# The first MoE's inner blocks 4 to 11 by pairs, four of them through seven half-depth products

## The chip, the cores and the metric

One core of a Trainium2 chip runs the whole program. The time is device microseconds (us) of one execution, and of several executions the median. TensorE (PE) does the matmuls, VectorE (DVE), ScalarE (ACT) and GpSimd (POOL) the rest, and SyncE (SP) starts the transfers.

## The reference

Attention over 2 batches of 8 heads of 768 positions (each position sees the first four and a window of 128) gives x, 1536 tokens by 512. Two feed-forward layers follow, whose weights are float64:

```python
def _moe_ref(x, w_gate, w_val, w_out) -> np.ndarray:
    g = x @ w_gate
    silu = g * (1.0 / (1.0 + np.exp(-g)))
    val = x @ w_val
    return (silu * val @ w_out).astype(np.float32)
...
def _moe2_ref(x, w_in, w_out, alpha) -> np.ndarray:
    h = x @ w_in
    g = np.maximum(h, 0.0) + alpha * np.minimum(h, 0.0)
    return (g @ w_out).astype(np.float32)
```

The inner size is 1536 in the first layer (12 inner blocks of 128) and 2048 in the second (16 inner blocks).

## The kernel before

**Arithmetic.** A product of full precision is made of three matmuls in a shorter format: high by high, high by low, low by high. So each operand is held as a high and a low tile. A product of 512 channels with one inner block for 512 tokens (`proj`) is 12 matmuls of 128x128 by 128x512; one of half the channels (`Duo.product`) is 6.

**Weights.** `Stream` turns float64 weights into high and low tiles, item by item (an item is 128x512 weights). SP loads raw words into one of RB = 3 buffers. `start` takes the upper words' magnitude on ACT (Abs, L548), `bits` puts the float32 together with three DVE operations (L584, L587, L590), ACT rounds it to the high tile wh (L593), and `low` subtracts for the low tile wl (L599), on POOL where `idle_pool` is set and on DVE elsewhere. Each item moves one step at each `tick`, and a tick follows each `yield` of a unit. An item's tiles lie in one of WB = 12 slots, with WX = 7 more while the third token block of chunk 0 and chunk 1 run. Items of kind 2 and 3 are sums of the two items ahead of them: four POOL operations on 128x256 halves (L566 to L569), wh by ACT (L572), wl by POOL.

**First layer.** `Moe1.unit(c, b)` does chunk c of four inner blocks for token block b of three (512 tokens each): for two blocks at a time the gate products with Silu on ACT, then the value products, each multiplied with its gate on DVE (`hid`, L718) and split into `hh` (ACT, L679) and `hl` (DVE, L680); then four output products of 12 matmuls, `po`, added to the running sum by DVE (L742; in chunk 0 copied by ACT). Units (0, 0) and (0, 1) run beside attention, whose DVE order is fixed by the code (`tc.manual_schedule`).

**Second layer.** `Duo` takes its inner blocks by pairs. After a plain first pair, the products with token blocks 0 and 1 follow a scheme of 2x2 blocks (halves of the channels, two inner blocks or two token blocks) with seven products in place of eight: it needs sums of weights (kinds 2 and 3) and sums of the tokens' values t1 to t4 (`Duo.sums`, DVE on 128x1024, L827). ACT copies some products out of PSUM (`keep`, L850), and DVE adds them to others (L855). Token block 2 is done plainly. Then 12 output products of 6 matmuls follow (`pf`, L947 to L949, added by DVE at L954).

**Order.** A scheduler sets each engine's order from the order of the code and estimated times; each engine then runs its list in order, held up only by what an instruction needs. PSUM has eight banks of 128x512.

Of the kernel before, what the change touches and what calls it, by code (L numbers as in the profile page):

```python
# [35 lines left out]
WB = 12  # L36
WX = 7
RB = 3
VB = 6
LAG = 2  # L40
ORDER = ((0, 3), (1, 2), (4, 5))
# [18 lines left out]
def setup(nc, tc, ctx, g):  # L60
    const = ctx.enter_context(tc.tile_pool(name="const", bufs=1))
    g.const = const
    g.ident = const.tile([P, P], F32, name="ident")
    for nm in ("alpha", "sig", "sal", "sdn"):
        setattr(g, nm, const.tile([P, NF2], F32, name=nm))
    g.mask_a = const.tile([P, KW], F32, name="mask_a")
    g.mask_b = const.tile([P, KW], F32, name="mask_b")
    g.mask_0 = const.tile([P, P], F32, name="mask_0")
    g.mask_1 = const.tile([P, 2 * P], F32, name="mask_1")
    g.above = const.tile([P, P], I32, name="above")  # L70
    g.zero = const.tile([P, T], mybir.dt.bfloat16, name="zero")
# [397 lines left out]
def weight_pools(nc, tc, ctx, g, sfx):  # L469
# [31 lines left out]
class Stream:  # L501
# [49 lines left out]
    def bits(self):  # L551
# [9 lines left out]
        if kind > 1:  # L561
# [10 lines left out]
            nc.scalar.activation(wh, m, AF.Copy)  # L572
# [5 lines left out]
        if slot is None or g.exact:  # L578
            nc.vector.tensor_scalar(out=m, in0=m, scalar1=WMAX, scalar2=-WMAX, op0=ALU.min, op1=ALU.max)
            w2 = g.w2_p.tile([P, KD * P], F32, tag="w2", name="w_2")  # L580
            sign, wi = mi, w2.bitcast(I32)
# [49 lines left out]
def moe1_seq(wg, wv, wo):  # L631
    seq = []
    for c in range(NF1 // CHUNK):
# [17 lines left out]
def duo_seq(wi, wo):  # L651

    seq = []
    for f in range(0, NF2, DUO):
        fs = range(f, f + DUO)
        seq += [(0, wi, x, DOWN, 3 * NF1 + x) for x in fs]
        seq += [(2, None, 0, None, None), (3, None, 0, None, None)] if f else []
# [153 lines left out]
class Duo:  # L811
# [3 lines left out]
    def __init__(self, nc, g, st, base, ys, out, halves):  # L815
        self.nc, self.g, self.st, self.base, self.ys, self.out, self.halves = nc, g, st, base, ys, out, halves
        self.accs = {}

    def sums(self, a0, a1):

        nc, g = self.nc, self.g
        a, b, c, d = a0[:, 0:2], a0[:, 2:4], a1[:, 0:2], a1[:, 2:4]
        t1, t2, t4 = ([half(g.x_p2, n + z) for z in "hl"] for n in ("t1", "t2", "t4"))
        self.ts = ts = [t1, t2, [y[0] for y in self.ys[1]], t4]

        def sub(out, x, y):
            return lambda: nc.vector.tensor_tensor(out=out, in0=x, in1=y, op=ALU.subtract)  # L827

        def split(x, t):
            return lambda: split_hidden(nc, x, *t)  # L830

        self.last = split(c, ts[2])
        return [sub(a, c, a), sub(c, d, c), split(a, ts[0]), sub(d, d, a), split(d, ts[1]), sub(b, b, d), split(b, ts[3])]
# [14 lines left out]
    def keep(self, ps, tag):  # L848
        t = self.g.u_p.tile([P, T], F32, tag=tag, name=tag)
        self.nc.scalar.activation(t, ps, AF.Copy)  # L850
        return t

    def add(self, ps, u):
        t = self.g.t_p.tile([P, T], F32, tag="hid", name="sum")
        self.nc.vector.tensor_tensor(out=t, in0=ps, in1=u, op=ALU.add)  # L855
        return t

    def bend(self, src, f, pair, inplace=False):
        nc, g = self.nc, self.g
        if inplace:  # L860
            hid = src
            nc.vector.scalar_tensor_tensor(
                out=hid, in0=src, scalar=g.alpha[:, f:f + 1], in1=src, op0=ALU.mult, op1=ALU.max
            )
        else:
            neg = g.t_p.tile([P, T], F32, tag="sg", name="neg")
            nc.scalar.activation(neg, src, AF.Copy, scale=g.alpha[:, f:f + 1])
            hid = g.t_p.tile([P, T], F32, tag="hid", name="hid2")
            nc.vector.tensor_tensor(out=hid, in0=src, in1=neg, op=ALU.max)
        split_hidden(nc, hid, *(t[:, f % 2] for t in pair))  # L870

    def plain(self):

        st, w, hids = self.st, self.base, {}
        for b, pool in ((0, None), (1, self.g.h_p2), (2, None)):
            hids[b] = hidden_pair(self.g, pool)
            for r in range(DUO):
                ph = self.new("ph")
                proj(self.nc, ph, st.get(w + r), *self.ys[b])
                self.bend(ph, r, hids[b])  # L880
                yield
            if b == 1:
                self.last()
        st.done(DUO)
        for b in range(3):
            for _ in self.outputs(0, b, w + DUO, *hids[b]):
                yield
        st.done(DUO)

    def unit(self, c):  # L890
        nc, g, st = self.nc, self.g, self.st
        if c == 0:
            yield from self.plain()
            return
        w = self.base + 2 * DUO + (c - 1) * 3 * DUO
        f = c * DUO
        (y0h, y0l), (y1h, y1l), y2 = self.ys
        b11, b21, b22 = (y0h[0], y0l[0]), (y0h[1], y0l[1]), (y1h[1], y1l[1])
        t1, t2, t3, t4 = self.ts
        hids = {0: hidden_pair(g)}  # L900
        pa, pb, pc = self.new("pa"), self.new("pb"), self.new("pc")
        self.product(pa, w, 0, b11, True)
        p1 = self.keep(pa, "p1")
        yield
        self.product(pc, w, 1, b21, True)
        self.bend(self.add(pc, p1), f, hids[0], True)
        yield
        self.product(pb, w + 2, 0, t1, True)
        yield
        self.product(pa, w + 2, 1, t2, False)  # L910
        u2 = self.keep(pa, "u2")
        yield
        hids[2] = hidden_pair(g)
        hids[1] = hidden_pair(g, g.h_p2)
        for r in range(DUO):
            ph = self.new("ph")
            proj(nc, ph, st.get(w + r), *y2)
            self.bend(ph, f + r, hids[2])
            yield
            if r == 0:  # L920
                self.product(pa, w + 3, 0, t3, False)
                u3 = self.keep(pa, "u3")
                self.bend(self.add(pb, u3), f + 1, hids[1], True)
                yield
        self.product(pa, w + 1, 1, t4, False)
        self.bend(pa, f + 1, hids[0])
        yield
        self.product(pb, w + 3, 1, b22, False)
        self.bend(self.add(pb, u2), f, hids[1], True)
# [243 lines left out]
```

## Time and profile before

| | |
|---|---|
| median of 3 runs | 670.21 us (668.44 to 671.4) |
| profiled execution, its own time | 670.04 us |
| its span in the trace | 668.0 us |
| what lies around the span | 2.04 us |
| PE busy | 648.6 us, 3056 matmuls |
| DVE / ACT / POOL busy | 430.7 / 306.6 / 158.6 us |
| mean granted clock of TensorE | 0.983 of full speed |

The span runs from the first to the last recorded instruction of the core; own time is that of the same execution measured outside. The busy time of an engine is the sum of its instructions; it says which engine is nearly full, and the waits and the chain that ended last say whether it also sets the time.

### The profile page before, as it was taken

Reading aid. Unit: us, or ns where it says so; the run is one execution under the profiler, and the core shown is the slowest. Engines: PE = TensorE matmul, PEld = TensorE weight load, DVE = VectorE, ACT = ScalarE, POOL = GpSimd, SP = SyncE. Lnnn points to the kernel's source line nnn. Section 1 sums busy time; section 2 is a strip of 40 time slices with the busy share of each in tenths; the row PEclk is TensorE's granted clock in tenths of the full one; section 3 lists DMA queues with packets and bytes.
Section 4 is the critical chain, followed back from the end, with each engine's and each line's share of the span. In section 5 each row is a group of like instructions: output and inputs, shape, how many; then the busy total and the mean of one; then the engine's idle time right before and its main releaser. Section 6 shows DMA issues by size and latency. Waiting matters only on the chain.

```text
span 668.0 us, 8689 instructions
## 1 busy us (share of the span) xinstructions
PE 648.6 (97%) x3056; PEld 511.6 (77%) x3056; DVE 430.7 (64%) x915; ACT 306.6 (46%) x714; POOL 158.6 (24%) x203
## 2 busy tenths in 40 slices
PE   8879899999999999999999999999999999999996
PEld 4547566767788888888888888888888888888884
DVE  6897967355189852227432699938686969684654
ACT  4768755666366622024222356655344353533040
POOL 3547644334100000000000004614334251420000
PEclk8879899999999999999999999999999999999999
DMA  8754444100045620001300023222121303100005
GB/s 288 221 171 149 154 136 149 32 13 1 1 135 181 187 97 0 1 1 40 118 0 1 0 94 99 82 66 72 64 65 62 95 31 95 32 1 1 0 1 193
DMA packets 37203, 52.29 MB, mean 78 GB/s; under 512 B 4384, under 2 KB 28960, under 8 KB 37152
## 3 DMA queue, kind: packets, MB, share of 16 engines
q1 hardware_dynamic: 34944, 51.65, 24.2%
q8 instruction: 26, 0.43, 0.3%
q10 hardware_dynamic: 2208, 0.01, 0.2%
q14 instruction: 25, 0.20, 0.1%
HBM read 48.51 MB, written 3.15 MB: 77 GB/s over the span
## 4 chain that ended last, share of the span: by engine, by line
PE 88%; DVE 5%; ACT 3%; issue 1%; DMA 1%; POOL 1%; ACTq 0%; POOLq 0%
PE pf L947 7%; PE pf L948 7%; PE pf L949 7%; PE pa L841 6%; PE po L735 5%; PE pg L666 5%; PE po L736 5%; PE po L737 5%; PE pv L666 5%; PE pg L667 5%; PE pg L668 5%; PE pv L668 5%; PE pv L667 5%; PE pb L841 3%; PE ph L667 3%; PE ph L666 3%
## 5 line engine op out<-in xcount | busy, mean ns | idle before, releaser
L599 POOL TENSOR_TENSOR wl<-w_m,wh 128x512 fp32r<-128x512 f32 x44 | 57.9, 1322 | 99.1 <-ACT wh L593 87.1
L593 ACT ACTIVATE wh<-w_m 128x512 fp32r<-128x512 f32 x68 | 42.6, 629 | 76.9 <-PE pf L949 45.4
L947 PE MATMUL pf<-wh,hh 128*128 128x512 f32 x192 | 74.7, 389 | 0.0
L948 PE MATMUL pf<-wl,hh 128*128 128x512 f32 x192 | 74.7, 389 | 0.0
L679 ACT ACTIVATE hh<-hid 128x512 fp32r<-128x512 f32 x63 | 39.9, 633 | 66.7 <-DVE hid L718 51.7
L566 POOL TENSOR_TENSOR w_raw<-w_m 128x256 f32<-128x256 f32 x7 | 5.9, 840 | 253.0 <-DVE w_m L590 226.9
L949 PE MATMUL pf<-wh,hl 128*128 128x512 f32 x192 | 62.0, 389 | 0.0
L954 DVE TENSOR_TENSOR acc<-pf,acc 128x512 f32<-128x512 f32 x84 | 54.4, 681 | 11.4 <-PE pf L949 10.7
L718 DVE TENSOR_TENSOR hid<-pv,sg 128x512 f32<-128x512 f32 x36 | 24.7, 687 | 56.6 <-PE pv L668 56.5
L680 DVE TENSOR_TENSOR hl<-hid,hh 128x512 fp32r<-128x512 f32 x63 | 47.4, 754 | 20.7 <-ACT hh L679 20.3
L666 PE MATMUL pg<-xh,wh 128*128 128x512 f32 x144 | 57.5, 400 | 0.0
L666 PE MATMUL pv<-xh,wh 128*128 128x512 f32 x144 | 56.9, 395 | 0.0
L548 ACT ACTIVATE w_m<-w_raw 128x512 f32<-128x512 f32 x68 | 45.8, 674 | 24.0 <-DVE wl L599 9.6
L667 PE MATMUL pg<-xl,wh 128*128 128x512 f32 x144 | 56.7, 393 | 0.0
L668 PE MATMUL pg<-xh,wl 128*128 128x512 f32 x144 | 56.6, 393 | 0.0
L735 PE MATMUL po<-hh,wh 128*128 128x512 f32 x144 | 56.4, 395 | 0.0
L668 PE MATMUL pv<-xh,wl 128*128 128x512 f32 x144 | 56.1, 390 | 0.0
L667 PE MATMUL pv<-xl,wh 128*128 128x512 f32 x144 | 56.1, 389 | 0.0
L736 PE MATMUL po<-hh,wl 128*128 128x512 f32 x144 | 56.0, 390 | 0.0
L737 PE MATMUL po<-hl,wh 128*128 128x512 f32 x144 | 53.3, 390 | 0.0
L587 DVE SCALAR_TENSOR_TENSOR w_m<-w_raw,w_m 128x512 int32<-128x512 int32 x68 | 50.0, 736 | 1.1
L590 DVE SCALAR_TENSOR_TENSOR w_m<-w_raw,w_m 128x512 uint32<-128x512 uint32 x68 | 49.0, 723 | 0.6
(161 smaller groups left out, 1400.6 us busy)
## 6 DMA issues: line engine op xcount, KB each, us to landing
w_raw<-in_moe_w_out SPq DMA_DIRECT2D x28, 512.0 KB, 3.4
w_raw<-in_moe_w_in SPq DMA_DIRECT2D x16, 512.0 KB, 3.8
w_raw<-in_moe_w_gate SPq DMA_DIRECT2D x12, 512.0 KB, 4.4
w_raw<-in_moe_w_val SPq DMA_DIRECT2D x12, 512.0 KB, 4.4
th<-in_qk SPq DMA_DIRECT2D x16, 336.0 KB, 3.3
vr<-in_v SPq DMA_DIRECT2D x16, 192.0 KB, 2.6
out<-acc SPq DMA_DIRECT2D x12, 256.0 KB, 2.5
th<-in_qk SPq DMA_DIRECT2D x8, 256.0 KB, 5.1
```

Of the source, the lines that this page charges most:

```text
L599: eng.tensor_tensor(out=wl, in0=m, in1=wh, op=ALU.subtract)
L666: nc.tensor.matmul(ps, wh[:, c], chan(xh, kk), start=(kk == 0), stop=False)
L667: nc.tensor.matmul(ps, wh[:, c], chan(xl, kk), start=False, stop=False)
L668: nc.tensor.matmul(ps, wl[:, c], chan(xh, kk), start=False, stop=(kk == KD - 1))
L735: nc.tensor.matmul(ps, wh[:, mc], hh, start=(x == 0), stop=False)
L736: nc.tensor.matmul(ps, wl[:, mc], hh, start=False, stop=False)
L737: nc.tensor.matmul(ps, wh[:, mc], hl, start=False, stop=(x == CHUNK - 1))
L841: self.nc.tensor.matmul(ps, a[:, c], m[:, k], start=(start and k == 0 and y == 0), stop=(k == 1 and y == 2), skip_group_check=True)
L947: nc.tensor.matmul(ps, hh[:, x, ts], wh, start=(x == 0), stop=False)
L948: nc.tensor.matmul(ps, hh[:, x, ts], wl, start=False, stop=False)
L949: nc.tensor.matmul(ps, hl[:, x, ts], wh, start=False, stop=(x == DUO - 1))
L954: nc.vector.tensor_tensor(out=av, in0=ps, in1=av, op=ALU.add)
```

## The change

Chunk 0 of the first layer (blocks 0 to 3) stays. Blocks 4 to 11 are done by pairs (`Duo1`): 4, 5 and 10, 11 plainly, 6, 7 and 8, 9 with the seven products, once for the gates and once for the values (`Chain`, which the second layer now uses too, in the order ORDER7). This needs x's sums t1 to t4 once (`Duo1.sums`, taken up one by one at the yields of the third token block of chunk 0), and two items more (kinds 2 and 3) ahead of each of the four chains. The outputs are added up by pairs, so each of the 12 sums of a token block takes its additions pair by pair. The high tiles of the weights' sums come from POOL instead of ACT, in both layers, and `idle_pool` stays set, so the low tiles of the first layer's later items come from POOL too. Slots are 10, with 2 more for chunk 0's items and 2 more from the last pair on. `g.soon()` gives a higher priority in the scheduler to what follows a product: the copies and additions of the chains, Silu, multiply, split, and the additions of the outputs. Masks and scratch tiles of attention move to pools that close with it. The diff, cut to its core (the second layer's class is the same as before but for `Chain` and `g.soon()`):

```diff
+ORDER7 = (1, 2, 5, 6, 8, 7, 9, 4, 3)
-WB = 12
-WX = 7
+WB = 10
 RB = 3
+WA = 2
...
-            nc.scalar.activation(wh, m, AF.Copy)
+            nc.gpsimd.tensor_copy(wh, m)
             self.halves = (i, m, wh, wl)
...
+SUMS = [(2, None, 0, None, None), (3, None, 0, None, None)]
+def duo1_seq(wg, wv, wo):
+    seq = []
+    for f in range(CHUNK, NF1, DUO):
+        fs = range(f, f + DUO)
+        more = SUMS if CHUNK < f < NF1 - DUO else []
+        seq += [(0, wg, x, DOWN, x) for x in fs] + more
+        seq += [(0, wv, x, DOWN, NF1 + x) for x in fs] + more
+        seq += [(1, wo, x, DOWN, 2 * NF1 + x) for x in fs]
+    return seq
...
+        with self.g.soon():
+            self.nc.scalar.activation(t, ps, AF.Copy)
...
+class Chain:
+    def __init__(self, duo, w, ops, more, room, sink):
+        self.duo, self.w, self.ops, self.more, self.room, self.sink = duo, w, ops, more, room, sink
+    def plus(self, ps, u, b, r):
+        t = self.room(b, r)
+        with self.duo.g.soon():
+            self.duo.nc.vector.tensor_tensor(out=t, in0=ps, in1=u, op=ALU.add)
+        self.sink(b, r, t, True)
+    def step(self, x):
+        d, w = self.duo, self.w
+        b11, b21, b22, t1, t2, t3, t4 = self.ops
+        if x == 1:
+            self.a = d.new("pa")
+            d.product(self.a, w, 0, b11, True)
+            self.p1 = d.keep(self.a, "u1")
+        elif x == 2:
+            ps = d.new("pc")
+            d.product(ps, w, 1, b21, True)
+            self.plus(ps, self.p1, 0, 0)
+        elif x == 6:
+            d.product(self.a, w + 2, 1, t2, False)
+            self.u2 = d.keep(self.a, "u2")
+        elif x == 5:
+            self.b = d.new("pb")
+            d.product(self.b, w + 2, 0, t1, True)
+        elif x == 7:
+            d.product(self.a, w + 3, 0, t3, False)
+            self.plus(self.b, d.keep(self.a, "u1"), 1, 1)
+        elif x == 4:
+            d.product(self.a, w + 1, 1, t4, False)
+            self.sink(0, 1, self.a, False)
+        elif x == 3:
+            d.product(self.b, w + 3, 1, b22, False)
+            self.plus(self.b, self.u2, 1, 0)
+        else:
+            ps = d.new("ph")
+            proj(d.nc, ps, d.st.get(w + x - 8), *self.more)
+            self.sink(2, x - 8, ps, False)
...
+    def sums(self):
         nc, g = self.nc, self.g
+        (x0h, x0l), (x1h, x1l), _ = self.xs
+        a, c, d = ((x[0], y[0]) for x, y in ((x0h, x0l), (x1h, x1l), (x1h[1:], x1l[1:])))
+        b = x0h[1], x0l[1]
+        t1, t2, t4 = ([half(g.x_p2, n + z) for z in "hl"] for n in ("t1", "t2", "t4"))
+        self.ops = [a, b, d, t1, t2, None, t4]
+        u, v = (g.h_p2.tile([P, 2, T], F32, tag=z, name="tsum") for z in ("hh", "hl"))
+        return [
+            self.sub(u, c[0], a[0]), self.add(u, u, c[1]), self.sub(u, u, a[1]),
+            self.sub(v, d[0], u), self.split(u, t1), self.add(v, v, d[1]),
+            self.sub(u, b[0], v), self.split(v, t2), self.add(u, u, b[1]),
+            self.sub(v, d[0], c[0]), self.split(u, t4), self.add(v, v, d[1]), self.sub(v, v, c[1]), lambda: self.third(v),
+        ]
+    def third(self, v):
+        self.ops[5] = [half(self.g.x_p3, "t3" + z) for z in "hl"]
+        split_hidden(self.nc, v, *self.ops[5])
...
+        def gate(b, r, src, own):
+            t = src if own else room_g(b, r)
+            with g.soon():
+                nc.scalar.activation(t, src, AF.Silu)
+            gates[b, r] = t
+        def room_v(b, r):
+            return g.t_p.tile([P, T], F32, tag="hid", name="hid")
+        def value(b, r, src, own):
+            hid = src if own else room_v(b, r)
+            with g.soon():
+                nc.vector.tensor_tensor(out=hid, in0=src, in1=gates[b, r], op=ALU.mult)
+                split_hidden(nc, hid, *(t[:, r] for t in pairs[b]))
...
+        last = (NF1 - CHUNK) // DUO - 1
+        w = self.base + (3 * DUO + (c - 1) * 5 * DUO if c else 0)
+        if c in (0, last):
+            yield from self.plain(w, c == last)
+            return
+        pairs = self.pairs()
+        room_g, gate, room_v, value = self.sinks(pairs)
+        for i, room, sink in ((0, room_g, gate), (2 * DUO, room_v, value)):
+            chain = self.chain(w + i, self.ops, self.xs[2], room, sink)
+            yield from chain.steps(ORDER7)
+            chain.done()
+        for b in (2, 0, 1):
+            for m in range(KD):
+                self.output(b, m, w + 4 * DUO, *pairs[b])
+                yield
+        self.st.done(DUO)
+    def output(self, b, m, w, hh, hl, y=None):
+        nc, st = self.nc, self.st
+        mc = slice(m * P, (m + 1) * P)
+        ps = self.new("po")
+        for x in range(DUO):
+            wh, wl = st.get(w + x)
+            nc.tensor.matmul(ps, wh[:, mc], hh[:, x], start=(x == 0), stop=False)
+            nc.tensor.matmul(ps, wl[:, mc], hh[:, x], start=False, stop=False)
+            nc.tensor.matmul(ps, wh[:, mc], hl[:, x], start=False, stop=(x == DUO - 1))
+        av = self.accs[b][0][:, m]
+        with self.g.soon():
+            nc.vector.tensor_tensor(out=av, in0=ps, in1=av, op=ALU.add)
+            if y:
+                split_hidden(nc, av, *(chan(t, m) for t in y))
...
+    seq = moe1_seq(w_gate, w_val, w_out, 1) + duo1_seq(w_gate, w_val, w_out)
+    base = len(seq)
+    add_pool(nc, tc, early, g.w_ps, "w_pa", WA, "right")
...
+    for nm, bufs in (("x_p2", 6), ("u_p", 1), ("h_p2", 1), ("t_p2", 4)):
+        setattr(g, nm, ctx.enter_context(tc.tile_pool(name=nm, bufs=bufs)))
+    st.idle_pool = True
...
+    later.extend(d1.sums())
+    run([m1.unit(0, 2)])
+    assert g.w_ps.pop()[1] == WA
+    early.close()
+    last = (NF1 - CHUNK) // DUO - 1
     with ExitStack() as inner:
-        add_pool(nc, tc, inner, g.w_ps, "w_p2", WX)
-        run([m1.unit(0, 2)] + [m1.unit(1, b) for b in range(NPASS)])
-        assert g.w_ps.pop()[1] == WX
-    for nm, bufs in (("x_p2", 6), ("u_p", 1), ("h_p2", 1)):
-        setattr(g, nm, ctx.enter_context(tc.tile_pool(name=nm, bufs=bufs)))
-    run([m1.unit(2, b) for b in range(NPASS)])
-    st.idle_pool = True
-    run([m2.unit(c) for c in range(NF2 // DUO)])
-    assert asked
+        g.x_p3 = inner.enter_context(tc.tile_pool(name="x_p3", bufs=2, side="right"))
+        run([d1.unit(c) for c in range(last)])
+        assert not later
+    add_pool(nc, tc, ctx, g.w_ps, "w_p3", WA, "right")
+    st.own = range(base - 3 * DUO, len(st.seq))
+    run([d1.unit(last)] + [d2.unit(c, ys) for c in range(NF2 // DUO)])
...
+        g.soon = lambda: tc.high_priority(offset=SOON)
```

DVE at the end of attention and the start of unit (0, 2): `xl` is the low part of attention's last values, `tsum` the sums of x, `t1l` and `t2l` their low parts, `w_m` and `wl` the weights. Before:

```order
L1019 TENSOR_TENSOR xl<-xp,xh 128x256 x3
L599 TENSOR_TENSOR wl<-w_m,wh 128x512 x2
L584 TENSOR_SCALAR w_m<-w_m 128x512
L587 SCALAR_TENSOR_TENSOR w_m<-w_raw,w_m 128x512
L584 TENSOR_SCALAR w_m<-w_m 128x512
L590 SCALAR_TENSOR_TENSOR w_m<-w_raw,w_m 128x512
L587 SCALAR_TENSOR_TENSOR w_m<-w_raw,w_m 128x512
L590 SCALAR_TENSOR_TENSOR w_m<-w_raw,w_m 128x512
L599 TENSOR_TENSOR wl<-w_m,wh 128x512 x2
L584 TENSOR_SCALAR w_m<-w_m 128x512
L718 TENSOR_TENSOR hid<-pv,sg 128x512
```

With the change (line numbers there are of the changed kernel):

```order
L1182 TENSOR_TENSOR xl<-xp,xh 128x256 x2
L833 TENSOR_TENSOR tsum<-xh 128x1024
L1182 TENSOR_TENSOR xl<-xp,xh 128x256
L836 TENSOR_TENSOR tsum<-tsum,xl 128x1024
L833 TENSOR_TENSOR tsum<-tsum,xl 128x1024
L833 TENSOR_TENSOR tsum<-xh,tsum 128x1024
L693 TENSOR_TENSOR t1l<-tsum,t1h 128x1024
L836 TENSOR_TENSOR tsum<-tsum,xl 128x1024
L833 TENSOR_TENSOR tsum<-xh,tsum 128x1024
L731 TENSOR_TENSOR hid<-pv,sg 128x512
L836 TENSOR_TENSOR tsum<-tsum,xl 128x1024
L693 TENSOR_TENSOR t2l<-tsum,t2h 128x1024
```

In this place the weights' bit operations and low tiles gave way to the sums of x; the bit operations stand behind them, and the low tiles have left DVE's list.

POOL behind its last work for attention (the rows `pt<-pt`). Before, it had nothing until the second layer's first sums of weights:

```order
L295 AFFINE_SELECT pt<-pt 128x2x128 x2
L566 TENSOR_TENSOR w_raw<-w_m 128x256
L567 TENSOR_TENSOR w_raw<-w_raw,w_m 128x256
L568 TENSOR_TENSOR w_m<-w_m 128x256
L569 TENSOR_TENSOR w_m<-w_m,w_raw 128x256
L599 TENSOR_TENSOR wl<-w_m,wh 128x512 x3
```

With the change:

```order
L296 AFFINE_SELECT pt<-pt 128x2x128 x2
L599 TENSOR_TENSOR wl<-w_m,wh 128x512 x7
L567 TENSOR_TENSOR w_raw<-w_m 128x256
L599 TENSOR_TENSOR wl<-w_m,wh 128x512
L568 TENSOR_TENSOR w_raw<-w_raw,w_m 128x256
L569 TENSOR_TENSOR w_m<-w_m 128x256
L570 TENSOR_TENSOR w_m<-w_m,w_raw 128x256
L573 CAST wh<-w_raw 128x512
L573 CAST wh<-w_m 128x512
```

Low tiles and four groups of sums of the first layer now stand ahead of the second layer's.

ACT from the copies of unit (0, 2)'s outputs (`acc`) on: Abs of an item writes `w_m,wsum`, `sg` is Silu, `hh` the high part of the product of gate and value. Before:

```order
L740 ACTIVATE acc_2255<-po 128x512
L548 ACTIVATE w_m,wsum<-w_raw 128x512
L593 ACTIVATE wh<-w_m 128x512
L710 ACTIVATE sg<-pg 128x512
L548 ACTIVATE w_m,wsum<-w_raw 128x512
L593 ACTIVATE wh<-w_m 128x512
L710 ACTIVATE sg<-pg 128x512
L548 ACTIVATE w_m,wsum<-w_raw 128x512
L593 ACTIVATE wh<-w_m 128x512
L679 ACTIVATE hh<-hid 128x512
```

With the change:

```order
L753 ACTIVATE acc_2227<-po 128x512 x3
L593 ACTIVATE wh<-w_m 128x512 x2
L957 ACTIVATE sg<-ph 128x512 x2
L549 ACTIVATE w_m,wsum<-w_raw 128x512
L692 ACTIVATE hh<-hid 128x512 x2
L549 ACTIVATE w_m,wsum<-w_raw 128x512
L957 ACTIVATE sg<-ph 128x512 x2
L692 ACTIVATE hh<-hid 128x512 x2
```

Between two Abs there now stand the high parts and Silus of a pair, and one Abs still stands ahead of each of the first high parts.

## Rows read from the trace of the kernel before

**Rows 1.** The page's first part: span, and each engine's busy time, share, instructions.

```profile
span 668.0 us, 8689 instructions
...
PE 648.6 (97%) x3056; PEld 511.6 (77%) x3056; DVE 430.7 (64%) x915; ACT 306.6 (46%) x714; POOL 158.6 (24%) x203
```

**Rows 2.** All waits of PE between 100 and 700 us (total, times, longest).

```profile
PE ps_s L224 <- ACT pr L234: 0.8, 1, 0.8
PE xp L320 <- POOL pt L295: 0.4, 1, 0.4
```

**Rows 3.** Busy time by stage (PE, PEld, DVE, ACT, POOL; then clock, DMA, GB/s).

```profile
0.00:182.00 182.00, 169.01 (x941) 114.98 (x942) 114.81 (x414) 113.72 (x352) 82.76 (x137) 0.94 0.38 121
182.00:215.00 33.00, 33.00 (x148) 27.28 (x147) 29.58 (x53) 22.20 (x47) 0.00 (x0) 1.00 0.46 146
215.00:345.00 130.00, 130.00 (x575) 107.67 (x574) 63.21 (x104) 38.02 (x73) 0.00 (x0) 1.00 0.19 61
345.00:400.00 55.00, 55.00 (x245) 45.53 (x244) 32.10 (x48) 21.07 (x37) 0.05 (x1) 1.00 0.08 24
400.00:661.00 261.00, 261.00 (x1154) 216.02 (x1153) 190.30 (x299) 111.58 (x207) 75.77 (x66) 1.00 0.19 60
```

**Rows 4.** The chain that ended last, 600 us on (start, length, instruction).

```profile
630.31 1.36 PE pa L841 x6
...
661.62 0.69 DVE acc L954
```

**Rows 5.** Groups of instructions by line (busy, mean ns, idle before and releaser).

```profile
L599 POOL TENSOR_TENSOR wl<-w_m,wh 128x512 fp32r<-128x512 f32 x44 | 57.9, 1322 | 99.1 <-ACT wh L593 87.1 <-PE pf L949 11.4
...
L599 DVE TENSOR_TENSOR wl<-w_m,wh 128x512 fp32r<-128x512 f32 x31 | 21.0, 685 | 2.1 <-ACT wh L593 1.9
L742 DVE TENSOR_TENSOR acc<-po,acc 128x512 f32<-128x512 f32 x24 | 15.8, 686 | 24.1 <-PE po L737 23.8
L295 POOL TENSOR_SCALAR_AFFINE_SELECT pt<-pt 128x256 f32<-128x256 f32 x32 | 13.7, 450 | 0.3
...
L855 DVE TENSOR_TENSOR sum<-pb,u 128x512 f32<-128x512 f32 x14 | 9.6, 686 | 6.7 <-ACT u L850 6.7
...
L850 ACT ACTIVATE u<-pa 128x512 f32<-128x512 f32 x14 | 8.3, 593 | 9.2 <-PE pa L841 9.2
L568 POOL TENSOR_TENSOR w_m<-w_m 128x256 f32<-128x256 f32 x7 | 8.1, 1154 | 0.2
...
L567 POOL TENSOR_TENSOR w_raw<-w_raw,w_m 128x256 f32<-128x256 f32 x7 | 6.6, 938 | 0.1
L566 POOL TENSOR_TENSOR w_raw<-w_m 128x256 f32<-128x256 f32 x7 | 5.9, 840 | 253.0 <-DVE w_m L590 226.9 <-PE pa L841 26.1
L569 POOL TENSOR_TENSOR w_m<-w_m,w_raw 128x256 f32<-128x256 f32 x7 | 5.7, 808 | 0.0
...
L827 DVE TENSOR_TENSOR acc<-acc,acc 128x1024 f32<-128x1024 f32 x3 | 3.7, 1218 | 0.0
```

**Rows 6.** DVE's groups between 182 and 215 us, the columns as in 5.

```profile
L587 DVE SCALAR_TENSOR_TENSOR w_m<-w_raw,w_m 128x512 int32<-128x512 int32 x11 | 7.6, 689 | 0.2
L590 DVE SCALAR_TENSOR_TENSOR w_m<-w_raw,w_m 128x512 uint32<-128x512 uint32 x10 | 6.8, 684 | 0.0
L584 DVE TENSOR_SCALAR w_m<-w_m 128x512 int32<-128x512 int32 x11 | 4.7, 424 | 1.9 <-ACT w_m L548 1.9
```

**Rows 7.** Timeline around 428 us (start, length, instruction, idle before and releaser).

```profile
425.74 0.67 ACT L548 ACTIVATE w_m<-w_raw 128x512 f32<-128x512 f32 x1 [2.17 <-POOL w_m L568]
...
427.62 1.82 POOL L599 TENSOR_TENSOR wl<-w_raw,wh 128x512 fp32r<-128x512 f32 x1 [1.21 <-PE pf L949]
...
428.20 1.79 DVE L590 SCALAR_TENSOR_TENSOR w_m<-w_raw,w_m 128x512 uint32<-128x512 uint32 x1
```

**Rows 8.** Timeline around 454 us, the columns as in 7.

```profile
452.99 0.63 ACT L679 ACTIVATE hh<-hid 128x512 fp32r<-128x512 f32 x1 [0.76 <-DVE hid L869]
...
454.58 0.39 PE L947 MATMUL pf<-wh,hh 128*128 128x512 f32 x1
```

More of the change, by code (lines that the diff above doesn't have):

```diff
@@ L579, in bits @@
             nc.vector.tensor_scalar(out=m, in0=m, scalar1=WMAX, scalar2=-WMAX, op0=ALU.min, op1=ALU.max)
[L580 to L581 removed]
+            sign, wi = mi, hi
         else:
@@ L628, in done, with moe1_seq @@
             self.n_done += 1
-def moe1_seq(wg, wv, wo):
+def moe1_seq(wg, wv, wo, chunks=NF1 // CHUNK):
     seq = []
-    for c in range(NF1 // CHUNK):
+    for c in range(chunks):
         fs = range(c * CHUNK, (c + 1) * CHUNK)
@@ L811, with __init__, sub, add @@
 class Duo:
[L815 to L833, printed above, removed]
+    def __init__(self, nc, g, st):
+        self.nc, self.g, self.st = nc, g, st
+    def sub(self, out, x, y):
+        return lambda: self.nc.vector.tensor_tensor(out=out, in0=x, in1=y, op=ALU.subtract)
+    def add(self, out, x, y):
+        return lambda: self.nc.vector.tensor_tensor(out=out, in0=x, in1=y, op=ALU.add)
+    def split(self, x, t):
+        return lambda: split_hidden(self.nc, x, *t)
     def product(self, ps, w, r, x, start):
@@ L849, in keep @@
         t = self.g.u_p.tile([P, T], F32, tag=tag, name=tag)
-        self.nc.scalar.activation(t, ps, AF.Copy)
-        return t
[L853 to L858, printed above, removed]
-        nc, g = self.nc, self.g
[L860 to L864, printed above, removed]
-        else:
[L866 to L929, printed above, removed]
-        st.done(2 * DUO)
-        yield
-        for b in (2, 0, 1):
-            for _ in self.outputs(c, b, w + 2 * DUO, *hids[b]):
-                yield
@@ new lines, in keep, with chain, pairs, steps @@
+        with self.g.soon():
+            self.nc.scalar.activation(t, ps, AF.Copy)
+        return t
+    def chain(self, w, ops, more, room, sink):
+        return Chain(self, w, ops, more, room, sink)
+    def pairs(self):
+        g = self.g
+        return {b: hidden_pair(g, pool) for b, pool in ((0, g.h_p), (2, g.h_p), (1, g.h_p2))}
+class Chain:
[36 more added lines that the diff above has]
+            self.sink(2, x - 8, ps, False)
+    def steps(self, order):
+        for x in order:
+            self.step(x)
+            yield
+    def done(self):
+        self.duo.st.done(2 * DUO)
```

139 lines of the change are left out of this document (115 added, 24 removed).

## The prediction, made before the changed kernel ran

> **What bounds the kernel now.** The page's first part comes first: PE is busy for 648.6 of 668.0 us, DVE for 430.7 [rows 1]. A share alone does not say that an engine sets the end, so the waits of PE are next: between 100 and 700 us there are two, 1.2 us in all, both on work of attention [rows 2]. The table by stage says the same from the other side: from 182 to 661 us PE's busy time equals the length of each stretch, at a granted clock of 1.00 in each (2.4 GHz), while DVE has spare time in all of them: 3.4 us of 33 just behind attention, 67 of 130 later, 71 of 261 in the second layer [rows 3]. The chain that ended last runs from 600 us to 661.6 through PE's products and then one addition on DVE [rows 4]; from its end, 662.3, to 668.0 the output's last transfers take 5.7 us, which the change does not touch. So a matmul fewer behind attention is worth its time, as long as nothing that PE needs comes later than PE now would ask for it. The sum has two kinds of terms: matmuls, and waits that do not exist yet.
>
> **What the change takes from PE.** A product of six matmuls takes 1.36 us in the chain [rows 4], 0.227 us for each. A plain pair's gates (or values) for two token blocks are eight half products of blocks (each six matmuls, as 4 full products are 48 matmuls); the scheme does seven. There are two such pairs, each with a chain for the gates and one for the values: 4 x 6 = 24 matmuls fewer, 4 x 1.36 = 5.4 us. Outputs by pairs are as many matmuls as by four: 12 products of 12 become 24 of 6. The span without new waits would be 668.0 - 5.4 = 662.6 us.
>
> **What it adds elsewhere, over the whole kernel.** DVE loses the 31 low tiles, 21.0 us by their row. It gains 24 more additions of outputs at 0.686 (16.5 us), 12 additions in the chains at 0.686 (8.2 us), and 14 operations on 128x1024 for x's sums at 1.22 (17.1 us; the second layer's same sums stand for them) [rows 5]: some 21 us more. ACT gets 12 copies out of PSUM at 0.593 (7.1 us) and loses the high tiles of the weights' sums to POOL. POOL gets 31 low tiles at 1.32 (41 us), four groups of sums at 0.84 + 0.94 + 1.15 + 0.81 = 3.74 and two low tiles each (4 x 6.4 = 25.5 us), and 22 copies in the second and first layer [rows 5]. Such a copy is not in the trace. Its bounds: POOL's affine select, with one input too, is 450 ns for 256 columns, 0.9 for 512; the low tile, with two inputs, 1.32. I take 1.0, as it has one input (22 us in all). Each is hidden where the engine has time, and by stage that is so: a unit with two chains has 204 matmuls (in each chain 42 of the seven products and 24 of token block 2, and 72 for the outputs), 46.2 us on PE; in it DVE has six items at 0.42 + 2 x 0.69 = 1.8 [rows 6] and 30 operations near 0.69 (six additions in the chains, six products with the gate, six low parts, twelve output sums), 31.6 us, and POOL two groups for sums at 3.74 + 2 x 1.0 + 2 x 1.32 = 8.4 and six low tiles, 24.7 us. If this cover were gone, as it would be for operations that PE waits for one by one, each would cost its own 0.7 to 1.3 us.
>
> **The stretch behind attention** is the one place where the cover is thin, and the third term of the sum comes from there. From attention's last product on (about 181 us) PE has unit (0, 2): 192 matmuls until it asks for the high part `hh` of the first pair, 192 x 0.227 = 43.5 us. In DVE's new order there stand ahead of that: 14 operations of x's sums (17.1 us), 8 of `hid` and `hl` at 0.69 (5.5), 7 shifts at 0.42 (2.9), 12 other bit operations at 0.69 (8.3), and the last part of x (0.4) [rows 5, 6]: 34.2 us, so 9.3 spare. POOL, which did nothing there before [rows 3], now does 8 low tiles (10.6 us) and three of four operations of the first sums (0.84 + 0.94 + 1.15 = 2.9), 13.5 us in the same time. And rows show that the two hold each other up: at 428 us a bit operation on DVE that takes 0.68 elsewhere took 1.79 beside a low tile on POOL, which itself took 1.82 in place of 1.32 [rows 5, 7].
> What does that make of the time? From below nothing: 9.3 us are spare, and a little waiting is taken up. From above: if each of POOL's operations stood ahead of one on DVE and held it for all of its length, DVE would need 34.2 + 13.5 = 47.7 us, 4.2 more than PE has. In the second layer, where POOL was busy for 76 us, PE never waited for DVE, and at its tightest place `hh` was done 0.96 us before the matmul that reads it [rows 3, 8]: the scheduler's order leaves little slack, but enough. I take 0.8 us, nearer to the lower end, since the trace's only stretch with both engines busy had no wait at all. By the Trainium skill ("SBUF — State Buffer", section "Who interferes with whom") a VectorE operation with two inputs in SBUF and a GpSimd operation that reads SBUF block each other for a whole instruction, whichever issues second waiting. The pair at 428 us agrees. Taken wholly, as if VectorE always issued second, it gives the upper end, 4.2 us of wait; the spare 9.3 us without it gives none.
>
> **ACT and SP.** ACT is busy for under half of the span [rows 1]. Queued behind a waiting Abs there are the pair's Silu, `keep` and `hh`, and PE waits for those: one Abs stands ahead of the first `hh`, and waits for the buffer that POOL's third operation of the sums frees. Before, ACT was held so at 425.7 us for 2.17 us, and PE did not wait [rows 2, 7]. I cost it at nothing inside a pair, and keep the other end as a rival. SP issues the same loads as before into 10 slots in place of 12 and 7. A unit of 46 us needs six loads, DMA is below a fifth busy behind 215 us [rows 3], and each item is converted in 1.8 us of DVE, so nothing for it. The higher priorities cost no instruction; they move additions ahead of conversions, which is what the slack at 454 us wants, and I count no gain, since PE had no wait to lose.
>
> **Sum.** 668.0 - 5.4 + 0.8 = 663.4 us of span; with the 2.04 us around it 665.4 for the profiled execution; the median of the runs shown is 0.2 above that execution, so 665.6 us.
>
> **Rivals.**
> *First stretch late.* DVE and POOL hold each other up by most of the bound and PE waits 1.5 to 4.2 us at the first pair's outputs or value chain: 670.2 - 5.4 + 1.5 to 4.2 = 666.3 to 669.0 us. For it: 13.5 us of POOL beside 34.2 of DVE, and the 1.79 us row. Against it: 9.3 us spare, and not every operation meets another. The rule of the Trainium skill named above, in the same section of "SBUF — State Buffer", is this rival's mechanism.
> *Slower.* In each of the four chains ACT is held by an Abs behind POOL's whole group for a chain (8.4 us, more if DVE holds POOL), with `keep` and Silu queued behind it, and PSUM fills while PE waits. It decides from 2.2 us a chain on (8.8 in all: 5.4 of gain and 3.35 beyond). With 2.3 each the time is 670.2 - 5.4 + 9.2 = 674.0 us. For it: the 2.17 us at 425.7, and two such groups in each unit with chains, where the second layer had one. Against it: PE had no wait from it at seven such groups before.
> *The saved time is not on the path.* With ten slots weights come late and PE stands where it would have multiplied: 670.2 us. For it only the fewer slots; against it the spare DMA and DVE time of 215 to 345 us [rows 3].
>
> **How the numbers follow.** Chances: the forecast (waits up to 1.5 us, 664.8 to 666.3 us) 0.62, the first stretch 0.27, slower 0.06, not on the path 0.05. The range goes from 664.0 (no wait is 664.8; 0.8 is left for the median, whose three runs lie 3 us apart) to 669.3 (the first rival's upper end and 0.3), and leaves the last two out. What a measurement can tell from no change is about 0.5%, 3.35 us: 666.9 us or less is faster, so 2.1 us of waits or more make it "same". All but a little of the forecast (0.58) and a small part of the first rival (0.02) are faster: 0.60. The rest of these and the third rival are same: 0.34. Slower: 0.06.
>
> **What the profile of the changed kernel would show.** PE with 3032 matmuls and some 643 us busy; no PE waits between 182 and 655 us but one or two near 215 to 230 us, by DVE or ACT (`hl`, `hh` of the first pair). DVE's bit operations there above 0.69 us in the mean; if they are 0.69, the two do not meet and the wait is nil. POOL's copies near 1.0 us, and its busy time near 158.6 + 41 + 25.5 + 22 = 247 us. The prediction is wrong if PE waits at each chain for ACT or POOL (rival two), if PE waits for `wl` or `wh` (rival three), or if POOL's copy is far over 1.3 us, which would make POOL's group longer than a chain's 15 us.

## The result: 0.7% slower

Six runs of the changed kernel have a median of 673.96 us (673.11 to 677.26), six of the kernel before beside them 669.38 us; the ratio is 1.007 (95% interval 1.0048 to 1.0092). Forecast were 665.6 us and a range from 664.0 to 669.3. The profiled execution took 673.82 us, its span is 672.1 us.

The page's first part, of the changed kernel, against [rows 1]:

```profile
span 672.1 us, 8796 instructions
...
PE 645.8 (96%) x3032; PEld 506.1 (75%) x3032; DVE 473.8 (71%) x933; ACT 308.7 (46%) x716; POOL 243.5 (36%) x281
```

The 24 matmuls are gone as forecast, and POOL's 243.5 us are near the 247 worked out; DVE has 22 us more than its terms gave. PE's waits between 176 and 672 us, where [rows 2] had none behind attention (total, times, longest):

```profile
PE po L1018 <- ACT hh L692: 4.5, 2, 2.5
PE pa L847 <- ACT u L857: 1.1, 2, 0.7
```

Two waits are for the high part `hh`, in the first and in the last plain pair. The first, on the timeline (start, length, instruction, idle before and releaser):

```profile
222.41 0.73 POOL L569 TENSOR_TENSOR w_m<-w_m 128x256 f32<-128x256 f32 x1
223.18 0.66 ACT L549 ACTIVATE w_m<-w_raw 128x512 f32<-128x512 f32 x1 [3.00 <-POOL w_m L569]
223.62 0.39 PE L681 MATMUL ph<-xh,wl 128*128 128x512 f32 x1
223.97 0.71 DVE L584 TENSOR_SCALAR w_m<-w_m 128x512 int32<-128x512 int32 x1 [5.43 <-ACT w_m L549]
224.60 0.68 DVE L966 TENSOR_TENSOR hid<-ph,sg 128x512 f32<-128x512 f32 x1
225.31 0.63 ACT L692 ACTIVATE hh<-hid 128x512 fp32r<-128x512 f32 x1 [1.38 <-DVE hid L966]
226.00 0.50 PE L1018 MATMUL po<-hh,wh 128*128 128x512 f32 x1 [1.99 <-ACT hh L692]
```

Read upwards from the last row: PE's next matmul starts 2.38 us after the one before, 2.15 more than its usual step of 0.227, waiting for `hh` (225.31). `hh` waits for the product with the gate (224.60), which in DVE's list stands behind the shift at 223.97, an operation on the weights. DVE had been idle for 5.43 us there: the shift waits for ACT's Abs, and Abs for POOL's third operation on a sum of weights, which frees one of two buffers. The second wait:

```profile
391.97 1.89 DVE L1023 TENSOR_TENSOR acc<-po,acc 128x512 f32<-128x512 f32 x3 [4.72 <-PE po L1020]
...
396.11 2.60 DVE L693 TENSOR_TENSOR yl<-acc,yh 128x512 fp32r<-128x512 f32 x2
396.55 1.61 POOL L599 TENSOR_TENSOR wl<-w_m,wh 128x512 fp32r<-128x512 f32 x1
398.63 1.21 DVE L693 TENSOR_TENSOR t1l<-acc,t1h 128x1024 fp32r<-128x1024 f32 x1
399.25 1.74 POOL L599 TENSOR_TENSOR wl<-w_m,wh 128x512 fp32r<-128x512 f32 x1 [1.10 <-ACT wh L593]
399.76 2.31 DVE L833 TENSOR_TENSOR acc<-acc 128x1024 f32<-128x1024 f32 x1
401.06 0.39 PE L681 MATMUL ph<-xh,wl 128*128 128x512 f32 x1
402.60 0.68 DVE L966 TENSOR_TENSOR hid<-ph,sg 128x512 f32<-128x512 f32 x1
403.99 0.50 PE L1018 MATMUL po<-hh,wh 128*128 128x512 f32 x1 [2.54 <-ACT hh L692]
```

Here PE's matmul at 403.99 comes 2.70 us later than its usual step behind the one at 401.06. From 391.97 on DVE never stops (just before, it had stood idle for 4.72 us): the split of y and the second layer's sums stand ahead of the product with the gate, two low parts take 2.60 us in place of 1.37 and a sum 2.31 in place of 1.22, each beside a low tile on POOL. Behind this wait TensorE's granted clock fell to half, 1.2 GHz (by stretch: PE, PEld, DVE, ACT, POOL; then the clock):

```profile
404.00:405.00 1.00, 1.00 (x4) 0.85 (x5) 1.00 (x2) 0.22 (x1) 0.00 (x0) 1.00 0.00 0
405.00:406.00 1.00, 1.00 (x5) 0.80 (x4) 1.00 (x3) 1.00 (x2) 0.00 (x0) 0.76 0.00 0
406.00:408.00 2.00, 2.00 (x7) 1.51 (x6) 2.00 (x4) 0.36 (x1) 0.00 (x0) 0.50 0.00 0
```

That did not come with every such wait. In the run without the priority (below), whose engines run the same lists, the same 2.70 us ended at 405.3 us and the clock stayed at 1.00:

```profile
406.00:408.00 2.00, 2.00 (x11) 1.61 (x10) 2.00 (x5) 1.58 (x2) 0.00 (x0) 1.00 0.00 0
```

Over all traces of the changed kernel and of the experiments, it fell behind 7 of 23 waits of 2.0 to 3.3 us, and behind none of the shorter ones (1.7 us or less).

Something else is no wait at all. PE's matmuls follow at 0.227 us everywhere before, but in some stretches of the change, four long ones in the second layer among them, at 0.232 to 0.234 (called 0.233 from here on):

```profile
438.02 0.39 PE L1105 MATMUL pf<-wh,hh 128*128 128x512 f32 x1
438.25 0.40 PE L1106 MATMUL pf<-wl,hh 128*128 128x512 f32 x1
438.49 0.39 PE L1107 MATMUL pf<-wh,hl 128*128 128x512 f32 x1
...
439.19 0.40 PE L1107 MATMUL pf<-wh,hl 128*128 128x512 f32 x1
```

Five steps from 438.02 to 439.19 are 1.17 us, 0.234 each, at a clock of 1.00. So the span is made up: 662.6 (no waits) + 6.3 of waits (2.15, 2.70, and 0.62 and 0.85 on the chains' copies, each as the step between two starts less 0.227) + 1.6 for eight steps at the low clock (405.48 to 408.85) + 2.6 of steps at 0.233, summed over the trace, + 0.5 for the first steps behind waits - 1.1 for attention, which ended that much earlier in this execution, - 0.4 at the end: 672.1 us.

### The profile page after: what moved, and what is told of

Its sections match the earlier page's. It is cut to its first block, busy times and chain, and to the rows that moved or that the text cites. A ratio compares the mean times of both kernels' runs of the same rounds, so it can differ in the third digit from the quotient of the medians.

```text
span 672.1 us, 8796 instructions
## 1 busy us (share of the span) xinstructions
PE 645.8 (96%) x3032; PEld 506.1 (75%) x3032; DVE 473.8 (71%) x933; ACT 308.7 (46%) x716; POOL 243.5 (36%) x281
## 4 chain that ended last, share of the span: by engine, by line
PE 86%; DVE 5%; ACT 4%; POOL 2%; issue 1%; DMA 1%; SPq 0%; POOLq 0%; ACTq 0%
PE pa L847 9%; PE pf L1105 7%; PE pf L1107 7%; PE pf L1106 7%; PE ph L679 6%; PE ph L680 6%; PE ph L681 6%; PE pb L847 4%; PE po L1018 3%; PE po L1019 3%; PE po L1020 3%; PE xp L321 3%; PE ps_s L225 2%; PE pc L847 2%; PE po L748 2%; PE pg L679 2%
## 5 line engine op out<-in xcount | busy, mean ns | idle before, releaser
L599 POOL TENSOR_TENSOR wl<-w_m,wh 128x512 fp32r<-128x512 f32 x79 | 110.6, 1405 | 197.5 <-ACT wh L593 176.5
L584 DVE TENSOR_SCALAR w_m<-w_m 128x512 int32<-128x512 int32 x68 | 35.2, 517 | 37.8 <-ACT w_m L549 37.8
L680 PE MATMUL ph<-xl,wh 128*128 128x512 f32 x128 | 49.8, 389 | 0.0
L681 PE MATMUL ph<-xh,wl 128*128 128x512 f32 x128 | 49.8, 389 | 0.0
L679 PE MATMUL ph<-xh,wh 128*128 128x512 f32 x128 | 49.8, 389 | 0.0
L235 ACT ACTIVATE pr<-ps_s,nb 128x160 f32<-128x160 f32 (+2 forms) x96 | 38.0, 406 | 19.5 <-DVE nb L231 17.0
L225 PE MATMUL ps_s<-th 64*128 64x288 f32 (+2 forms) x192 | 39.2, 443 | 7.7 <-ACT pr L235 6.5
L1107 PEld LDWEIGHTS pf<-wh,hl 128*128 128x128 f32 x192 | 36.0, 188 | 8.1
L1106 PEld LDWEIGHTS pf<-wl,hh 128*128 128x128 f32 x192 | 36.0, 188 | 8.1
L1105 PEld LDWEIGHTS pf<-wh,hh 128*128 128x128 f32 x192 | 36.0, 188 | 8.0
```

Source lines behind the costliest of these rows:

```text
L599: eng.tensor_tensor(out=wl, in0=m, in1=wh, op=ALU.subtract)
L679: nc.tensor.matmul(ps, wh[:, c], chan(xh, kk), start=(kk == 0), stop=False)
L680: nc.tensor.matmul(ps, wh[:, c], chan(xl, kk), start=False, stop=False)
L681: nc.tensor.matmul(ps, wl[:, c], chan(xh, kk), start=False, stop=(kk == KD - 1))
L1105: nc.tensor.matmul(ps, hh[:, x, ts], wh, start=(x == 0), stop=False)
L1106: nc.tensor.matmul(ps, hh[:, x, ts], wl, start=False, stop=False)
```

## The experiments

All edits are to the changed kernel, but for one named below.

**Where tiles start.** The slow matmuls come where the work reads a tile of the pools at the right end of SBUF (`w_pa`, `x_p3`, `w_p3`), by the addresses of the built program; a trace shows no addresses. Two kernels put unused bytes at that end, 32 (8 columns) and 128:

```diff
+    pad = ctx.enter_context(tc.tile_pool(name="pad", bufs=1, side="right")).tile([P, 8], F32, name="pad")
+    nc.gpsimd.memset(pad, 0.0)
     early = ExitStack()
```

> The changed kernel with one unused tile of 32 bytes ahead of the pools at the right end of SBUF, so that their tiles (w_pa, x_p3, w_p3) start at 221120 in place of 221152 bytes, a multiple of 64. Theory (where these tiles start costs: matmuls that read them follow each other at 0.233 us, all others at 0.227): all at 0.227, the time 2.4 us below the changed kernel's, 674.0 to 671.6. Rival (the far end of SBUF is slow whatever the start, or something else runs in those stretches): 0.233 stays, 674.0.

> The same with 128 bytes, so that the tiles start at 221024: no multiple of 64, as all tiles of the changed kernel at the left end, which follow at 0.227. Theory, form one (a start 32 bytes ahead of a multiple of 2048 costs): 0.227 and 671.6. Form two (a start off a multiple of 64 costs, but at this end alone): 0.233 and 674.0. If both this and the 32-byte shift leave 0.233, it is the end of SBUF itself.

Measured: 674.38 us, ratio to before 1.0063 (1.0043 to 1.0083), and 671.87, 1.0035 (1.0019 to 1.005). 32 bytes change nothing, where 671.6 was forecast; 128 bring back 2.1 us, as form one of the second had it. So more than one start would have to be bad, if it were the start alone. A third kernel put 128 bytes into `const` at the left end instead, so that all tiles had the bad start:

> The changed kernel with 128 bytes put in at the left end of SBUF, so that all tiles that PE reads in the two layers start 32 bytes ahead of a multiple of 2048, as those at the right end did. Theory (that start costs 0.0066 us for each matmul): the 1800 or so that followed at 0.227 now follow at 0.233, 674.0 + 12 = 686. Rival (it is the right end of SBUF): 674.0.

Measured: 671.36, 1.0038 (1.002 to 1.0057): it became faster than the changed kernel, as neither forecast had it, and the steps at 0.233 were gone. The theory of a bad start fell. What fits is that the moving and the stationary tile start at different places. To test that, the kernel before the change got the same 128 bytes between its pools (opened just ahead of the slots' pool), and two more kernels other differences:

> The kernel before the change, with 128 unused bytes put between the tiles of x and of the product with the gate on one side and the weights' slots on the other. Theory (what costs is not where a tile starts but that the two tiles that PE reads together start at different places within 512 or 2048 bytes; here all were alike before): some 1800 of its matmuls follow at 0.233 in place of 0.227, 669.8 + 12 = 682. Rival (only tiles at SBUF's right end can be slow, or this kernel's matmuls cannot): 669.8.

> The changed kernel with 640 unused bytes at the right end: its tiles then start 512 bytes from the left end's place within 2048. Theory, form one (alike within 512 bytes is enough): matmuls that read them follow at 0.227. Form two (alike within 2048): 0.233, as in the changed kernel.

> The same with 192 bytes: the tiles start 64 bytes from the left end's place. Theory (starts that differ by 96 and by 128 bytes both cost): 0.233. Rival (a difference of 64 is free): 0.227.

Measured: 681.5 us, ratio 1.019 (1.0171 to 1.0209), forecast 682; and single runs of 671.04 and 672.48, to be read by their matmuls. The kernel before, so shifted, by stretch, and a product of six in its chain, against [rows 3, 4]:

```profile
215.00:345.00 130.00, 130.00 (x561) 105.41 (x560) 60.16 (x99) 36.94 (x72) 0.00 (x0) 1.00 0.18 58
```

```profile
607.42 1.39 PE pa L843 x6
608.81 1.41 PE pc L843 x6
```

561 matmuls in 130 us in place of 575, with no wait behind attention and a clock of 1.00: 2.5% of each matmul (0.232 in place of 0.226 us in this mean). The groups of matmuls of the outputs (mean ns last but one), of the changed kernel, then with 128, 640 and 192 bytes:

```profile
L1105 PE MATMUL pf<-wh,hh 128*128 128x512 f32 x192 | 75.3, 392 | 0.0
```

```profile
L1105 PE MATMUL pf<-wh,hh 128*128 128x512 f32 x192 | 74.7, 389 | 0.0
```

```profile
L1106 PE MATMUL pf<-wl,hh 128*128 128x512 f32 x192 | 74.7, 389 | 0.0
```

```profile
L1105 PE MATMUL pf<-wh,hh 128*128 128x512 f32 x192 | 75.2, 392 | 0.0
```

| difference of the two starts, bytes, within 2048 | step |
|---|---|
| 0 (before; 128 at either end) and 512 (640 bytes) | 0.227 |
| 64 (192 bytes), 96 (32 bytes), 128 (changed; before, apart) | 0.232 to 0.234 where such tiles meet |

**The first wait.** The first low tiles go back to DVE:

```diff
-    st.idle_pool = True
     asked = False
...
-        run([d1.unit(c) for c in range(last)])
+        run([d1.unit(0)])
+        st.idle_pool = True
+        run([d1.unit(c) for c in range(1, last)])
```

> The changed kernel with the low tiles on DVE from the end of attention to the end of the first pair (as before the change), on POOL behind that. Theory (the wait of 2.2 us at 224 us comes from POOL's list: the sums of weights stand behind and between low tiles, ACT's Abs waits for them, DVE's shift for Abs, and the product with the gate stands behind the shift): the wait falls under 0.5 us, 672.2. Rival, that of the prediction (DVE is too full in this stretch): some ten more operations of 0.69 us there make the wait longer, 674 to 678.

Measured: 672.71, 1.0042 (1.0026 to 1.0058); the wait is gone. The rival, the prediction's own picture of a full DVE, is out: more operations on DVE, no wait. Its timeline:

```profile
222.40 0.74 POOL L569 TENSOR_TENSOR w_m<-w_m 128x256 f32<-128x256 f32 x1
222.54 0.69 DVE L966 TENSOR_TENSOR hid<-ph,sg 128x512 f32<-128x512 f32 x1 [0.82 <-PE ph L681]
224.84 0.39 PE L681 MATMUL ph<-xh,wl 128*128 128x512 f32 x1
224.86 0.83 DVE L584 TENSOR_SCALAR w_m<-w_m 128x512 int32<-128x512 int32 x1
225.06 0.39 PE L1018 MATMUL po<-hh,wh 128*128 128x512 f32 x1
```

In DVE's list the product with the gate now stands ahead of the shift that waits for POOL. It starts 2.3 us ahead of PE's last matmul before `hh` (222.54, 224.84); in the changed kernel it started 1.0 us behind that matmul (224.60, 223.62). POOL's third operation stands at the same time of the span (222.40, 222.41), but attention ended 1.2 us later in this execution, so against PE it came 1.2 us earlier, which by itself could take that much of the 2.15. The mended kernel at the end of this section shows the order alone. There the third operation ends 0.15 us ahead of that matmul, later than the 0.5 of the changed kernel, the product stands ahead of the shift, and PE does not wait:

```profile
222.20 0.69 DVE L967 TENSOR_TENSOR hid<-ph,sg 128x512 f32<-128x512 f32 x1 [0.71 <-PE ph L682]
223.28 1.07 POOL L570 TENSOR_TENSOR w_m<-w_m 128x256 f32<-128x256 f32 x1
224.50 0.39 PE L682 MATMUL ph<-xh,wl 128*128 128x512 f32 x1
224.72 0.39 PE L1019 MATMUL po<-hh,wh 128*128 128x512 f32 x1
225.53 0.80 DVE L585 TENSOR_SCALAR w_m<-w_m 128x512 int32<-128x512 int32 x1
```

So DVE's order is what makes POOL's late operation cost anything.

**The layers' border.** Handing out the second layer's sums later (`len(ys) == 3` in place of 2 in `put_y`) did nothing to DVE's order there:

> The changed kernel with the second layer's sums of token values handed out from the end of the first layer's last pair on, not amid its third token block. Theory (the wait of 2.7 us at 401 us is DVE's queue: the product with the gate stands behind those sums): that wait goes, and the low granted clock that follows it (some 1.7 us): 674.0 - 4.4 = 669.6. Rival (DVE has as much to do either way, so the same wait comes a pair later): 673 to 674.

Measured: 673.26, 1.0055 (1.003 to 1.0081), with the wait of 2.70 us in place; all four engines ran the changed kernel's lists, so it says nothing on its theory. So an edge of order was added, and apart from it the last pair's low tiles put on DVE:

```diff
+    def behind(x):
+        def run():
+            with tc.issue_after(g.last_hid):
+                x()
+        return run
...
+            later.extend(behind(x) for x in d2.sums(ys, *old[:2]))
```

> The changed kernel with an edge of order on DVE: the second layer's sums of token values come behind the last pair's last product with the gate (in the run before, handing them out later did not move them on DVE, and the wait stayed). Theory (the wait of 2.7 us at 401 us is the product with the gate standing behind 128x1024 sums): the wait is gone, and the low clock behind it where it came: 674.0 - 2.7 - 0.5 to 2.1 = 669 to 671. Rival (DVE simply has too much to do around the two layers' border): the same wait one pair later, 673 to 674.

> The changed kernel with the low tiles of the last pair's stretch on DVE, the sums left ahead of the product with the gate. Theory (the queue is late there because POOL's low tiles held DVE: 1.2 us on two low parts of y and 1.1 us on a sum): DVE gets two operations of 0.69 us more but loses 2.3 us of being held; the wait falls from 2.7 to 1.8 us or less. Rival (the number of operations ahead of the product sets it): the wait grows to some 4.1 us.

Measured: 674.19, 1.0065 (1.0053 to 1.0078), and 672.95, 1.0055 (1.0035 to 1.0075). With the sums behind, the wait at 401 us is gone and two of 1.4 and 1.7 us come at 430. The rival named that place and nearly that time (673 to 674), but only a part of the reason: DVE's work held POOL there, and then DVE itself stood idle for 3.37 us. The timeline:

```profile
423.64 4.59 POOL L569 TENSOR_TENSOR w_m<-w_m 128x256 f32<-128x256 f32 x1
424.62 1.82 DVE L693 TENSOR_TENSOR yl<-acc,yh 128x512 fp32r<-128x512 f32 x2
426.35 1.29 DVE L693 TENSOR_TENSOR hl<-hid,hh 128x512 fp32r<-128x512 f32 x2
430.21 0.67 ACT L549 ACTIVATE w_m<-w_raw 128x512 f32<-128x512 f32 x1 [5.98 <-POOL wl L599]
431.01 0.56 DVE L584 TENSOR_SCALAR w_m<-w_m 128x512 int32<-128x512 int32 x1 [3.37 <-ACT w_m L549]
431.50 0.68 DVE L1064 TENSOR_TENSOR hid<-ph,neg 128x512 f32<-128x512 f32 x1
432.23 0.50 PE L1105 MATMUL pf<-wh,hh 128*128 128x512 f32 x1 [1.19 <-DVE hid L1064]
```

It is the first wait's chain again, and this time DVE held POOL: the same operation, 0.73 us in the rows of the first wait (1.15 in the mean of [rows 5]), took 4.59 beside a row of DVE operations, and ended 0.6 us behind the row's end. With the low tiles on DVE the wait at 401 us fell to 1.97 us, though two operations more stood ahead: the holding is part of that wait, near what the theory had (1.8 or less). The rest goes with the sums' place in the list, since the wait went with them.

**All three together, and the priority.**

> The 128-byte shift, the first low tiles on DVE and the sums behind the product with the gate together. Theory (three separate causes): their savings add up, 674.0 - 2.2 - 2.2 - 2.7 - 0.5 to 2.1 = 665 to 666.5, faster than before the change (669.4). Rival (one cause seen three times, or waits that pop up elsewhere): 669 or more.

> The changed kernel without the higher scheduler priority (the edit that puts what follows a product ahead of conversions). Theory (the priority is not the cause of the waits, and keeps the copies of the chains early): more waits on copies and products with the gate, 675 to 678. Rival (the priority caused the waits, by putting conversions late): 671 or less.

Measured: 669.63, 0.9997 (0.9988 to 1.0005), a miss: waits of 1.6 and 1.7 us at 428 and 431 us came, as behind the edge alone. Without the priority (`g.soon = ExitStack`): 673.99, 1.0074 (1.005 to 1.0097). The order of PE, DVE, ACT and POOL is the same row for row with and without it, so this part of the change moved nothing, and neither theory's mechanism is at work.

**A third buffer** for the item behind the sums of weights, with the 128 bytes, once with the sums behind the gate's product and once without:

```diff
+        free = getattr(g, "m_x", None) if i and self.seq[i - 1][0] == 3 else None
+        m = (free or g.raw_w).tile([P, KD * P], F32, tag="m", name="w_m")
```

> The changed kernel with the 128-byte shift, the sums behind the gate's product, and a third buffer for what follows the sums of weights, so that ACT's Abs does not wait until POOL's third operation frees one of the two; the low tiles stay on POOL. Theory (the waits at 224 and at 430 us are one chain: POOL's sums, Abs, DVE's shift, and the product with the gate behind the shift): both go, 674.0 - 2.2 - 2.2 - 2.7 = 667 or up to 1.5 less where the clock stays up. Rival (DVE is simply too full at the layers' border): some 3 us of waits stay there, 669 to 670.

> The 128-byte shift and the third buffer alone, the sums of token values where the change has them. Theory: the wait at 224 us goes, that at 401 us (sums on DVE ahead of the product with the gate, and held by POOL) stays at 2.7: 674.0 - 2.2 - 2.2 = 669.6. Rival (the shift behind Abs is not what holds the product at 224 us): 671.9, as with the shift of 128 bytes alone.

Measured: 671.59, 1.0029 (1.0013 to 1.0045), and 674.1, 1.0066 (1.0043 to 1.009), both above both of their forecasts. At 430 us the wait is gone (one of 0.14 us stands at 420). At 224 us it grew to 3.3 us: one Abs more ran ahead, the next one waited for the same third operation, and its shift again stood ahead of the product. So the buffer helps where one item follows the sums, not where two do. Both together, with the first low tiles on DVE:

> The changed kernel with the 128-byte shift, the sums behind the gate's product, the third buffer, and the first low tiles on DVE. Theory (each of the places found is a cause by itself): no wait at 224, 401 or 430 us, the two on copies stay (1.5 us), matmuls at 0.227: 669.8 - 5.4 + 1.5 + 1 = 667, faster than before the change by 0.4%. Rival (a wait taken away comes back further on, as behind 430 us in an earlier run): 669 to 671.

Measured: 666.09 us, ratio 0.9948 (0.9932 to 0.9964): faster than both kernels. Its page's first part, and its only waits of PE behind attention:

```profile
span 664.4 us, 8795 instructions
...
PE 642.7 (97%) x3032; PEld 506.4 (76%) x3032; DVE 474.9 (71%) x947; ACT 308.4 (46%) x716; POOL 225.3 (34%) x268
```

```profile
PE pa L848 <- ACT u L858: 1.1, 2, 0.7
```

## Why the prediction was wrong

- **What bounds the kernel, and the 5.4 us from PE: right.** The mended kernel's 666.1 us is 669.85 - 5.4 + 1.5 of waits left on the chains' copies, within 0.2.
- **The sum's third term was mis-sized, and its mechanism wrong.** The wait stands where it was looked for, at the first pair's `hh`, with 2.15 us in place of 0.8 (bounds 0 and 4.2). But DVE was not late with work. In the 43 us up to PE's wait it was busy for 35.9 us (34.2 were worked out for its operations) and POOL for 14.9 (13.5 worked out), and DVE stood idle for 5.43 us just ahead of the shift. That 2.15 lies within the first rival's 1.5 to 4.2 us is luck: its mechanism, a DVE held until it is late, is not what made PE wait.

```profile
181.00:224.00 43.00, 43.00 (x189) 35.11 (x187) 35.86 (x42) 22.55 (x41) 14.88 (x13) 1.00 0.20 62
```

- **The step that failed: "I cost it at nothing inside a pair"**, on ACT's Abs behind POOL's third operation. The text listed what is queued behind Abs on ACT (`keep`, Silu, `hh`), and not what waits for Abs on another engine: DVE's shift, with the product with the gate behind it. The evidence taken for nothing, the 2.17 us at 425.7 us [rows 7], was real, but there the product with the gate (`hid`) stood ahead of the shift in DVE's list:

```profile
425.03 0.68 DVE L869 TENSOR_TENSOR hid<-ph,neg 128x512 f32<-128x512 f32 x1
426.53 0.43 DVE L584 TENSOR_SCALAR w_m<-w_m 128x512 int32<-128x512 int32 x1 [0.82 <-ACT w_m L548]
```

- **A second step failed: "Each is hidden where the engine has time, and by stage that is so".** It put the layers' border at nothing, and PE waited 2.70 us there. A unit's mean of 31.6 us of DVE in 46 says nothing of 392 to 403 us, where the last output additions of a token block, the split of y and the second layer's sums stand in one row ahead of the product with the gate, right behind 4.72 us in which DVE had nothing to do. DVE's total was 22 us over the sum; low parts of 864 ns in the mean, where 0.69 was counted, fit a DVE held by POOL more often. The rival with POOL and DVE holding each other up had a part of the mechanism, in another place: with the low tiles off POOL the wait at 401 us was still 1.97 us.
- **What the steps were worth.** The span came out 8.7 us over the forecast's 663.4. The first step is 1.35 of that (2.15 for 0.8), and alone would have left the time inside the range. The border is 2.70, the copies 1.47, the matmuls at 0.233 us 2.6, the clock 1.6; the small terms of the sum above take 1.0 off.
- **The clock** was not thought of: 1.6 us in this execution. The wait alone does not bring it down, as the run without the priority shows; what else it takes stays open.
- **No rival knew the matmuls at 0.233 us**, 2.1 us by the medians, 2.6 by the steps. "Outputs by pairs are as many matmuls" counted them at one price.
- **The other rivals.** ACT held in each of the four chains did not come: 0.6 and 0.9 us on copies in the whole kernel. That this rival's 674.0 us is the measured median to within 0.1 is luck. Ten slots were enough. POOL's copy took 0.78 us in the mean of 22, below the lower bound of 0.9.

## What to carry to other kernels

A shared engine's late operation costs through the lists of all engines behind it: follow an inferred wait across engines until it meets something that PE reads, and look at what stands behind the waiting instruction there. A mean by stage does not show a border where two stages' work meets. When pools are moved, compare the starts of the tiles that PE reads together: differences of 64, 96 and 128 bytes cost here, 0 and 512 did not, and no others were run.

## What the runs showed of the hardware

Matmuls with a 512-column fp32r moving tile followed each other at 0.232 to 0.234 us in place of 0.227 where the moving tile and the stationary ones started 64, 96 or 128 bytes apart within 2048, and at 0.227 where they started alike or 512 apart (one run of that, and one of 64); 128 unused bytes cost a kernel without the change 1.9%. The Trainium skill ("SBUF — State Buffer", section "Who interferes with whom") lists PE's read ports for the moving operand and for weights as independent, and says that PE never waits on anyone. The measurement does not fit the first: with nothing else changed, the places of the two tiles set the step. Why, no run shows.
